# Linear attention, then a gated network, on one core: the first batch's key–value sums in four column groups and two banks, the last two slots in fresh banks by halves, and a new written-out order

## The chip, the cores and the metric

The kernel runs on one core of a Trainium2 chip. The core has TensorE (PE, matmuls; its weight loads are listed apart as PEld), VectorE (DVE), ScalarE (ACT), GpSimd (POOL) and SyncE (SP, which here only issues DMAs). Each takes its own instructions in order and waits on semaphores for the others. Matmuls write to PSUM, of which this kernel uses eight banks of 512 float32 per partition. The metric is the device time of one execution in microseconds (us); lower is better.

## The reference

Four batches, four heads, 1088 tokens, 32 features per head. `phi` makes 64 features of 32, as the outer product of two projections to 8. The attention is linear: per batch and head a 64×32 matrix `kv` and a vector `z` are summed over the tokens, then divided out per token. The result, 4352 tokens × 128, goes through a root-mean-square norm and a gated network with 1536 hidden units.

```python
def phi(x):
    a = np.einsum('rd,bhsd->bhsr', S1, x)
    b = np.einsum('rd,bhsd->bhsr', S2, x)
    return np.einsum('bhsi,bhsj->bhsij', a, b).reshape(*x.shape[:-1], r * r)
q_p, k_p = (phi(q), phi(k))
kv = np.einsum('bhsf,bhsd->bhfd', k_p, v)
z = np.sum(k_p, axis=2)
num = np.einsum('bhsf,bhfd->bhsd', q_p, kv)
den = np.einsum('bhsf,bhf->bhs', q_p, z)[..., None] + 1e-06
...
rms = np.sqrt(np.mean(x * x, axis=-1, keepdims=True) + 1e-06)
xn = x / rms * rms_g
g = xn @ w_gate
silu = g * (1.0 / (1.0 + np.exp(-g)))
val = xn @ w_val
return (silu * val @ w_out).astype(np.float32)
```

## The kernel before

The work is written as some 1280 small tasks, each with the engine or engines that can take it, what it reads and what it writes. The order in which the tasks go to the engines' queues is a list of task numbers (`ORDER`), and a string (`ON`) says which engine takes a task that has a choice. A planner (`Plan.follow`) walks this list with estimated durations, only to interleave the queues, to give out buffers, and to place a few filling matmuls at the start; on the chip each engine's queue has the order of the list, and semaphores do the rest.

**Keys** (`kside`, one call per batch). The keys of a batch come as nine tiles of 128 tokens, in groups (`K0` for batch 0, four groups; `KN` for the others, three). For a group, TensorE multiplies the keys with S1 and S2 (L479), the result is copied (`both` or `kab`, L306 and L307) and VectorE or GpSimd forms the features `phi` as a broadcast product (L434). Then the key–value matmuls (L490) add up `kv` and `z` over the tiles, with the features as the stationary operand and 34 columns of values as the moving one. In the batches listed in `QUARTERS` (1, 2, 3) a matmul takes 32 features, and four neighbours write to four column groups; batch 0 takes 64 features to a matmul. Two copies (`put`, L501 on VectorE, or L505 on ScalarE), one for the even heads and one for the odd, take the sums out of PSUM. In batch 0 the sums lie in the bank `o_ps`, in the others in one of the three `att` banks.

**Queries** (`qside`, one call per chunk of 512 tokens, the ninth of 256). Chunks 0 and 1 form their features with the tokens on the partitions (products L543, L434) and transpose them (L551); their products share one buffer, `at`, so chunk 1's wait for chunk 0's transposes. Later chunks go through DRAM (`far`, L571 to L600). Then come the numerator matmuls (L620), the denominator (L637, with EPS added), its reciprocal (L638), the division (L629), the mean of squares (L644), a root on GpSimd (`rstd`, L657), the scaling (`xn`, L660 or L677), a transpose (L664), and the split into `x_hi` (ScalarE, L667) and `x_lo` (VectorE, L670).

**Weights** (`weights`, one call for each of twelve blocks). The weights arrive as 64-bit words and are turned into float32 by an absolute value on ScalarE (L359) and four steps on VectorE (clamp L343, shift L347, sign L351, join `w_f` L354), and then split into `w_hi` (ScalarE, L415) and `w_lo` (VectorE or GpSimd, L418).

**Slots** (`slot`, one for each chunk and block, 108 in all). A slot is a gate and a value product of three passes each (L714), a silu (L723), a product `h` (L726), a split into `h_hi` and `h_lo` (L741, L744) and a down product of three passes into `o_ps` (L752). The first four slots and the last two (`LAST_EXACT`) take the down product in plain float32 (L733) instead. A chunk's twelve slots add up in the single bank `o_ps`; chunks 0 and 1 are done in two runs of six slots, the first of which is copied to `part` and added at the end (L768). The very last slot is worked in halves of 128 columns: gate and value products, `h`, down product, the copy to `o_sb` (L306, L307) and the store (L779; the first half from SyncE's queue, the second from ScalarE's).

The banks are: three `att`, one `o_ps`, two `g_ps` and two `v_ps`.

Of the kernel before, what the change touches and what calls it, by code (L numbers as in the profile page):

```python
# [12 lines left out]
U32 = mybir.dt.uint32  # L13
# [31 lines left out]
K0 = [(0, 1), (1, 4), (4, 6), (6, 9)]  # L45
# [39 lines left out]
"""  # L85
ON = (
    "daddpadadadadaadaaaaddappadpaddappappadpaddadpadpapdappadapadaaapaddaaddaapadapddaaddapdddddadpddpdddpdddddadddadaapddpd"
    "ddpdddpdppaaaddapppddpdppdppdaappddpppppppdpdpadappdpddddpddpdpdaadddddpdppddpdddpaaappapppppddpddppdppdddpddppad"
)
ATT = 3  # L90
QUARTERS = (1, 2, 3)
KEY1 = 1
KAB = 9
QHALVES = 1
# [7 lines left out]
STALLS = (4500, 900), (12000, 800)  # L102
# [33 lines left out]
class Plan:  # L136
# [32 lines left out]
    def follow(self, clock0, filler):  # L169
# [6 lines left out]
        for i in map(int, ORDER.split()):  # L176
# [28 lines left out]
            if e == "dma":  # L205
                wire = max(wire, at + FLIGHT) + w.lat
                while stalls and wire > stalls[0][0]:
                    wire += stalls.pop(0)[1]
                t.end = wire + SETTLE
                if not w.since:  # L210
                    landed.append(t.end)
            else:
                t.end = at + lat
# [45 lines left out]
def attention_then_glu(ctx, tc, kT, v, qT, sw, w, out):  # L259
# [128 lines left out]
    load(P * NB * 8, lambda: nc.scalar.dma_start(out=s_raw.rearrange("p n c -> p (n c)"), in_=sw.bitcast(U32)), ["s_raw"], since=740)  # L388
# [56 lines left out]
    def kside(b):  # L445
# [24 lines left out]
        for i, (lo, hi) in enumerate(groups):  # L470
            m, ab = hi - lo, gate(i % 2) if first or b <= KEY1 else ps("att", ATT)
            if not i:
                acc = ps("o_ps", 1) if first else ps("att", ATT)

# [9 lines left out]
            def kvmm(lo=lo, hi=hi):  # L484
                kvv = acc()[:, :2 * VA].rearrange("p (a x) -> p a x", x=VA)
                for t in range(lo, hi):
                    for h in range(H):
                        for f in range(0, F, wide):
                            r0 = (h % 2) * F + f
                            nc.tensor.matmul(  # L490
                                out=kvv[r0:r0 + wide, h // 2, :], lhsT=phi()[:, t, h * F + f:h * F + f + wide], rhs=vt()[:, t, h, :],
                                start=(t == 0 and h < 2), stop=(t == KT - 1), skip_group_check=True,
                            )
# [3 lines left out]
            pe(123 * m + 75 if b in QUARTERS else 232 * m + 10, kvmm, [(phi, i), *of(vt, vpieces, lo, hi)], [acc], None, 32 if b in QUARTERS else 64)  # L497
        for hh in range(2):
            def put(rows=slice(hh * F, (hh + 1) * F), xs=slice(hh * (D + 1), (hh + 1) * (D + 1))):
# [356 lines left out]
```

## Time and profile before

| | |
|---|---|
| median of three runs | 261.37 us (259.86 to 261.77) |
| the profiled execution, own time | 259.89 us |
| its span in the profile | 258.1 us |
| TensorE busy | 252.1 us, 98% of the span, 2120 matmuls |
| VectorE, ScalarE, GpSimd busy | 168.7 us, 147.8 us, 91.9 us |
| moved by DMA | 22.13 MB |
| TensorE clock granted | 0.998 |

All times in the profile count from the start of the span. A row of the timeline gives the start, the duration, the engine, the source line, the operation, what is written and read, the shapes, and how many equal neighbours were put together; in brackets stands how long the engine had been idle before it and what released it. Instructions of one engine overlap a little, so the step from one start to the next is often less than the duration. A row of stretches gives the borders, the length, and then the busy time and number of instructions of each engine shown (in the order PE, PEld, DVE, ACT, POOL), the granted clock, the share of DMA time and GB/s.

### The profile page before, as it was taken

The page shows a single profiled execution, that of the slowest core. Times are in us where ns is not written, and L with a number is a line of the kernel's source. Part 1 is how long each engine was busy: PE and PEld are TensorE (multiplying, and loading weights), DVE is VectorE, ACT ScalarE, POOL GpSimd, SP SyncE. Part 2 cuts the span into 40 slices and gives each one's busy share as a digit, 9 for nine tenths or more (in the row PEclk, how much of TensorE's full clock was granted, in tenths as well). Part 3 has the DMA queues.
Part 4 walks back from the last instruction along what each step waited for, and adds up shares of the span by engine and source line. Part 5 has one row for each costly group of instructions (what it writes and reads, how often), then busy time and mean ns, then how long its engine had stood idle before and what let it go on. Part 6 is the DMA issues. An engine that isn't in the chain of part 4 may idle for free.

```text
span 258.1 us, 5584 instructions
## 1 busy us (share of the span) xinstructions
PE 252.1 (98%) x2120; PEld 203.6 (79%) x2120; DVE 168.7 (65%) x396; ACT 147.8 (57%) x319; POOL 91.9 (36%) x93
## 2 busy tenths in 40 slices
PE   7899999999999999999999999999999999999995
PEld 4777688788788787887888788788888878888894
DVE  2999999998697675548466556456855655435552
ACT  3587798467644546544566617546645655547651
POOL 2331131204743303544525544531332126252421
PEclk9999999999999999999999999999999999999999
DMA  7969994064051161061151300000000100010010
GB/s 234 397 243 291 296 353 103 3 207 120 1 171 35 63 161 26 1 167 38 23 144 33 102 20 3 0 21 22 1 0 0 42 3 0 0 41 3 0 41 22
DMA packets 13498, 22.13 MB, mean 86 GB/s; under 512 B 1952, under 2 KB 5024, under 8 KB 13472
## 3 DMA queue, kind: packets, MB, share of 16 engines
q1 hardware_dynamic: 13040, 21.52, 26.8%
q8 instruction: 16, 0.26, 0.4%
q10 hardware_dynamic: 432, 0.26, 0.3%
q14 instruction: 10, 0.08, 0.1%
HBM read 18.69 MB, written 3.08 MB: 84 GB/s over the span
## 4 chain that ended last, share of the span: by engine, by line
PE 94%; DVE 3%; DMA 1%; issue 1%; ACT 0%
PE g_ps L714 28%; PE v_ps L714 28%; PE o_ps L752 26%; PE att L620 3%; PE o_ps L733 2%; PE att L664 2%; PE att L490 2%; DMA s_raw<-sw 1%; PE att L571 1%; PE att L479 1%; DVE at L434 1%; PE att L543 0%; PE g_ps L479 0%; DVE w_tmp L343 0%; DVE w_tmp L347 0%
## 5 line engine op out<-in xcount | busy, mean ns | idle before, releaser
L726 DVE TENSOR_TENSOR h<-v_ps,s 128x512 f32<-128x512 f32 (+2 forms) x109 | 70.0, 652 | 48.2 <-PE v_ps L714 26.3
L744 POOL TENSOR_TENSOR h_lo<-h,h_hi 128x512 fp32r<-128x512 f32 (+1 forms) x48 | 58.9, 1235 | 92.0 <-ACT h_hi L741 42.7
L723 ACT ACTIVATE s<-g_ps 128x512 f32<-128x512 f32 (+1 forms) x108 | 60.7, 572 | 45.6 <-PE g_ps L714 30.8
L741 ACT CAST h_hi<-h 128x512 fp32r<-128x512 f32 (+1 forms) x102 | 59.8, 598 | 43.5 <-DVE h L726 39.2
L714 PE MATMUL v_ps<-x_hi,w_hi 128*128 128x512 f32 (+2 forms) x111 | 43.8, 394 | 0.0
L714 PE MATMUL g_ps<-x_hi,w_hi 128*128 128x512 f32 (+2 forms) x111 | 43.2, 389 | 0.0
L744 DVE TENSOR_TENSOR h_lo<-h,h_hi 128x512 fp32r<-128x512 f32 (+1 forms) x54 | 35.0, 661 | 11.8 <-POOL h_lo L744 5.9
L714 PE MATMUL g_ps<-x_lo,w_hi 128*128 128x512 f32 (+2 forms) x111 | 41.9, 378 | 0.0
L714 PE MATMUL v_ps<-x_hi,w_lo 128*128 128x512 f32 (+2 forms) x111 | 41.8, 377 | 0.0
L714 PE MATMUL v_ps<-x_lo,w_hi 128*128 128x512 f32 (+2 forms) x111 | 41.8, 377 | 0.0
L714 PE MATMUL g_ps<-x_hi,w_lo 128*128 128x512 f32 (+2 forms) x111 | 41.8, 377 | 0.0
L752 PE MATMUL o_ps<-h_hi,w_hi 128*128 128x512 f32 (+1 forms) x102 | 39.5, 387 | 0.0
L752 PE MATMUL o_ps<-h_lo,w_hi 128*128 128x512 f32 (+1 forms) x102 | 39.2, 384 | 0.0
L752 PE MATMUL o_ps<-h_hi,w_lo 128*128 128x512 f32 (+1 forms) x102 | 39.1, 383 | 0.0
L714 PEld LDWEIGHTS v_ps<-x_hi,w_hi 128*128 128x128 f32 x111 | 20.9, 188 | 5.5 <-DVE h L726 0.7
L714 PEld LDWEIGHTS g_ps<-x_hi,w_hi 128*128 128x128 f32 x111 | 20.9, 188 | 4.7 <-ACT w_hi L415 0.2
L714 PEld LDWEIGHTS v_ps<-x_hi,w_lo 128*128 128x128 f32 x111 | 20.9, 188 | 4.4 <-issue 0.7
L714 PEld LDWEIGHTS g_ps<-x_lo,w_hi 128*128 128x128 f32 x111 | 20.9, 188 | 4.2
L714 PEld LDWEIGHTS g_ps<-x_hi,w_lo 128*128 128x128 f32 x111 | 20.9, 188 | 4.2 <-DVE w_lo L418 0.2
L714 PEld LDWEIGHTS v_ps<-x_lo,w_hi 128*128 128x128 f32 x111 | 20.8, 188 | 4.2
L752 PEld LDWEIGHTS o_ps<-h_lo,w_hi 128*128 128x128 f32 x102 | 19.2, 188 | 4.0
L752 PEld LDWEIGHTS o_ps<-h_hi,w_hi 128*128 128x128 f32 x102 | 19.2, 188 | 3.8
(96 smaller groups left out, 255.4 us busy)
## 6 DMA issues: line engine op xcount, KB each, us to landing
w_raw<-w SPq DMA_DIRECT2D x12, 384.0 KB
bt<-far SPq DMA_DIRECT2D x24, 128.0 KB
at<-far SPq DMA_DIRECT2D x12, 256.0 KB
outT<-o_sb SPq DMA_DIRECT2D x8, 256.0 KB
q<-qT SPq DMA_DIRECT2D x7, 256.0 KB
vt<-v SPq DMA_DIRECT2D x4, 272.0 KB
kt<-kT SPq DMA_DIRECT2D x4, 256.0 KB
vt<-v SPq DMA_DIRECT2D x3, 340.0 KB
```

The costliest lines, as they stand in the source:

```text
L434: eng.tensor_tensor(out=out().rearrange("p t (h i j) -> p (t h) i j", h=H, i=R), in0=a[:, :, 0, :].unsqueeze(3).to_broadcast([P, m * H, R, ...
L479: nc.tensor.matmul(out=ab()[n0:rows.stop, (t - lo) * HALF:(t - lo + 1) * HALF], lhsT=kt()[:, s0:s0 + len(rows)], rhs=sblk, start=True, sto ...
L490: nc.tensor.matmul(out=kvv[r0:r0 + wide, h // 2, :], lhsT=phi()[:, t, h * F + f:h * F + f + wide], rhs=vt()[:, t, h, :], start=(t == 0 and ...
L620: nc.tensor.matmul(out=nv[n0:rows.stop, t, p, :], lhsT=phi()[:, p, l0:l0 + len(rows)], rhs=kvs[cut][:, p, :], start=True, stop=True,)
L664: nc.tensor.transpose(out=xt()[:, t * P:(t + 1) * P], in_=xn()[:, t, :], identity=ident)
L714: nc.tensor.matmul(out=acc()[:, cs], lhsT=wt[:, j, i3, :], rhs=x()[:, cs], start=(i == 0), stop=(i == 2))
L723: act(n, lambda: nc.scalar.activation(out=s()[:, :n], in_=gps()[:, :n], func=AF.Silu), cols(gps, whole[0]), [s])
L726: cs.stop - cs.start, lambda cs=cs: nc.vector.tensor_tensor(out=h()[:, cs], in0=vps()[:, cs], in1=s()[:, cs], op=ALU.mult),
L733: (cs.stop - cs.start) * 1.676 + 4, lambda cs=cs: nc.tensor.matmul(out=o_ps()[:, cs], lhsT=w_f[:, j, 2], rhs=h()[:, cs], start=first, stop ...
L741: act(n, lambda: nc.scalar.copy(out=h_hi()[:, :n], in_=h()[:, :n]), hs, [h_hi], True)
L744: eng.tensor_tensor(out=h_lo()[:, :n], in0=h()[:, :n], in1=h_hi().bitcast(F32)[:, :n], op=ALU.subtract)
L752: nc.tensor.matmul(out=o_ps()[:, :n], lhsT=wt[:, j, 2, :], rhs=x()[:, :n], start=first and i == 0, stop=last and i == 2,)
```

## The change

Batch 0 joins `QUARTERS`: its key–value matmuls take 32 features each, so there are twice as many. Its sums lie in two banks, `o_ps` for the even heads and an `att` bank for the odd ones; the two copies read one bank each. The groups of batch 0 are now tiles 0, 1 to 3, 4 to 6, 7 to 8 (the last two were 4 to 5 and 6 to 8).

The last chunk is done in two runs: slots 0 to 9 in `o_ps`, copied to `part`, and slots 10 and 11 in two `att` banks, one for each half of 128 columns. In both these slots `h` and the down product are made by halves; the gate and value products of the last slot are whole again. The end is two additions on VectorE (each a half from its own bank plus the same half of `part`) instead of two copies.

The denominator may go to ScalarE (10 of 17 do). `ORDER` and `ON` are new throughout; the planner's constants for stalls and for one load change with them, which only touches the interleaving. Read by task names, the order of the first slots' preparation is:

| engine | before | after |
|---|---|---|
| TensorE, key–value part | products of q1.2; kv tiles 0, 1–3, 4–5, 6–8; numerators of chunk 0; transposes of q1 | transposes of q0; kv 0, 1–3; transpose of q1.0; kv 4–6, 7–8; transpose of q1.2; numerators of chunk 0 |
| TensorE, ahead of the first slot | products of batch 1's keys and of tiles 0–2 of batch 2 | products of batch 1's keys |
| VectorE, up to the reciprocals | products q0.2, k0.0, q0.0, k0.2, k0.3, q1.2; weight 1 (clamp to join), copy out of kv, denominators, weight 0 (clamp, shift) | products q0.0, k0.1, k0.3, clamp 0, q1.0, k0.2; weights 0 and 1 (shift to join), weight 2 (clamp, shift) |
| ScalarE | one copy out of kv | both copies out of kv, denominators of chunks 0 and 1, each behind a rounding of a weight |
| loads from SyncE, after q1 | values, weight 1, values, values, weight 0, keys 1 | weight 0, values, weight 1, values, values, weight 2, keys 1 |

```diff
-K0 = [(0, 1), (1, 4), (4, 6), (6, 9)]
+K0 = [(0, 1), (1, 4), (4, 7), (7, 9)]
...
-QUARTERS = (1, 2, 3)
+QUARTERS = (0, 1, 2, 3)
 KEY1 = 1
 KAB = 9
+DEN_ACT = 60
...
-STALLS = (4500, 900), (12000, 800)
+STALLS = ((4500, 600), (12000, 400))
+SLATE = 650
...
                 acc = ps("o_ps", 1) if first else ps("att", ATT)
+                accs = [acc, ps("att", ATT) if first else acc]
...
-                kvv = acc()[:, :2 * VA].rearrange("p (a x) -> p a x", x=VA)
+                views = [a()[:, :2 * VA].rearrange("p (a x) -> p a x", x=VA) for a in accs]
                 for t in range(lo, hi):
                     for h in range(H):
+                        kvv = views[h % 2]
...
-            dve(20, lambda view=view, den=den: nc.vector.tensor_scalar_add(den(), view()[:, :, D:D + 1], EPS), [num], [den])
+            plan.add({
+                "dve": on_dve(20, lambda view=view, den=den: nc.vector.tensor_scalar_add(den(), view()[:, :, D:D + 1], EPS)),
+                "act": on_act(20, lambda view=view, den=den: nc.scalar.activation(
+                    out=den(), in_=view()[:, :, D:D + 1], func=AF.Copy, bias=EPS), against=DEN_ACT),
+            }, [num], [den])
...
-    runs = [(c, range(*r)) for r in ((0, CUT), (CUT, NJ)) for c in range(2)] + [(c, range(NJ)) for c in range(2, len(CHUNKS))]
+    runs = [(c, range(*r)) for r in ((0, CUT), (CUT, NJ)) for c in range(2)] + [(c, range(NJ)) for c in range(2, len(CHUNKS) - 1)]
+    runs += [(len(CHUNKS) - 1, r) for r in (range(NJ - LAST_EXACT), range(NJ - LAST_EXACT, NJ))]
...
-        up, rest_of = halves if t < 2 or not left else whole, halves if not left else whole
+        up, rest_of = halves if t < 2 else whole, halves if left < LAST_EXACT else whole
...
         if first:
-            acc_o[c] = ps("o_ps", 1)
-        o_ps = acc_o[c]
+            acc_o[c] = [ps("att", ATT) for _ in halves] if left < LAST_EXACT else [ps("o_ps", 1)]
+        o_ps, o_of = acc_o[c][0], acc_o[c]
...
-            for cs in rest_of:
+            for cs, o in zip(rest_of, o_of):
                 pe(
-                    (cs.stop - cs.start) * 1.676 + 4, lambda cs=cs: nc.tensor.matmul(
-                        out=o_ps()[:, cs], lhsT=w_f[:, j, 2], rhs=h()[:, cs], start=first, stop=last and cs.stop == n
+                    (cs.stop - cs.start) * 1.676 + 4, lambda cs=cs, o=o: nc.tensor.matmul(
+                        out=o()[:, cs], lhsT=w_f[:, j, 2], rhs=h()[:, cs], start=first, stop=last
...
-            dve(
-                n, lambda: nc.vector.tensor_tensor(out=o_sb()[:, :n], in0=o_ps()[:, :n], in1=part()[:, :n], op=ALU.add),
-                [*done, part], cols(o_sb, whole[0]),
-            )
+            for cs, o in zip(rest_of, o_of):
+                dve(
+                    cs.stop - cs.start, lambda cs=cs, o=o: nc.vector.tensor_tensor(out=o_sb()[:, cs], in0=o()[:, cs], in1=part()[:, cs], op=ALU.add),
+                    [*cols(o, cs), part], cols(o_sb, cs),
+                )
```

More of the change, by code (lines that the diff above doesn't have):

```diff
@@ L48 @@
 ORDER = """
[36 rows of a table removed]
[36 rows of a table added]
 """
 ON = (
-    "daddpadadadadaadaaaaddappadpaddappappadpaddadpadpapdappadapadaaapaddaaddaapadapddaaddapdddddadpddpdddpdddddadddadaapddpd"
-    "ddpdddpdppaaaddapppddpdppdppdaappddpppppppdpdpadappdpddddpddpdpdaadddddpdppddpdddpaaappapppppddpddppdppdddpddppad"
+    "ddpadadadaaadaapaaaaaaddappaddapdaddaddadpapdadpaddaddappapadapaaadaapaaaaddaadapapadadddaaaddpddpadppdpddpddddaddpapada"
+    "adddaadpddpdppddppaaadpadddppddppdppdpdaapdadappppddddddpdadapdadaddpddpppdpdpdadpdddapdpdppddppppadadpdadppppppddpddadp"
+    "pppddpdpa"
 )
 ATT = 3
-QUARTERS = (1, 2, 3)
+QUARTERS = (0, 1, 2, 3)
 KEY1 = 1
 KAB = 9
+DEN_ACT = 60
 QHALVES = 1
@@ L208, in follow @@
                     wire += stalls.pop(0)[1]
-                t.end = wire + SETTLE
+                t.end = wire + SETTLE + (w.occ - ISSUE if w.since else 0)
                 if not w.since:
@@ L386, in s_join @@
         nc.vector.tensor_tensor(out=sblk.bitcast(U32), in0=s_tmp.bitcast(U32), in1=s_top, op=ALU.bitwise_or)
-    load(P * NB * 8, lambda: nc.scalar.dma_start(out=s_raw.rearrange("p n c -> p (n c)"), in_=sw.bitcast(U32)), ["s_raw"], since=740)
+    plan.add({"dma": Way(
+        ISSUE + SLATE, P * NB * 8 / 320, lambda: nc.scalar.dma_start(out=s_raw.rearrange("p n c -> p (n c)"), in_=sw.bitcast(U32)), since=740
+    )}, (), ["s_raw"])
     plan.add({"act": Way(1500, 1500, lambda: nc.scalar.activation(out=spare, in_=mhalf, func=AF.Silu))}, (), ["table"])
@@ L496, in kside, with put, put_act @@
             product(lambda lo=lo, hi=hi: phi()[:, lo:hi], ab, m, [(phi, i)], not first)
-            pe(123 * m + 75 if b in QUARTERS else 232 * m + 10, kvmm, [(phi, i), *of(vt, vpieces, lo, hi)], [acc], None, 32 if b in QUARTERS else 64)
+            pe(123 * m + 75 if b in QUARTERS else 232 * m + 10, kvmm, [(phi, i), *of(vt, vpieces, lo, hi)], list(dict.fromkeys(accs)), None, 32 if b in QUARTERS else 64)
         for hh in range(2):
-            def put(rows=slice(hh * F, (hh + 1) * F), xs=slice(hh * (D + 1), (hh + 1) * (D + 1))):
+            def put(rows=slice(hh * F, (hh + 1) * F), xs=slice(hh * (D + 1), (hh + 1) * (D + 1)), acc=accs[hh]):
                 kvv = acc()[:, :2 * VA].rearrange("p (a x) -> p a x", x=VA)
                 nc.vector.tensor_copy(out=kv[rows, :, xs], in_=kvv[rows, :, :D + 1])
-            def put_act(rows=slice(hh * F, (hh + 1) * F), xs=slice(hh * (D + 1), (hh + 1) * (D + 1))):
+            def put_act(rows=slice(hh * F, (hh + 1) * F), xs=slice(hh * (D + 1), (hh + 1) * (D + 1)), acc=accs[hh]):
                 kvv = acc()[:, :2 * VA].rearrange("p (a x) -> p a x", x=VA)
                 nc.scalar.copy(out=kv[rows, :, xs], in_=kvv[rows, :, :D + 1])
-            plan.add({"dve": on_dve(2 * (D + 1), put), "act": on_act(2 * (D + 1), put_act, against=PUT_ACT)}, [acc], [("kv", b, hh)])
+            plan.add({"dve": on_dve(2 * (D + 1), put), "act": on_act(2 * (D + 1), put_act, against=PUT_ACT)}, [accs[hh]], [("kv", b, hh)])
     xs, qs = {}, {}
@@ L730, in slot @@
         if t < EXACT or left < LAST_EXACT:
-            for cs in rest_of:
+            for cs, o in zip(rest_of, o_of):
                 pe(
-                    (cs.stop - cs.start) * 1.676 + 4, lambda cs=cs: nc.tensor.matmul(
-                        out=o_ps()[:, cs], lhsT=w_f[:, j, 2], rhs=h()[:, cs], start=first, stop=last and cs.stop == n
+                    (cs.stop - cs.start) * 1.676 + 4, lambda cs=cs, o=o: nc.tensor.matmul(
+                        out=o()[:, cs], lhsT=w_f[:, j, 2], rhs=h()[:, cs], start=first, stop=last
                     ),
-                    [("w_f", j)] + cols(h, cs), [*cols(o_ps, cs), (o_ps, "group")], due, 0,
+                    [("w_f", j)] + cols(h, cs), [*cols(o, cs), (o, "group")], due, 0,
                 )
```

72 rows, old and new, of the table ORDER are left out of this document.

## The prediction

> **What bounds the kernel now.** I read the page's busy shares and its chain first, then the busy time of each engine in three stretches cut at two instants of the TensorE timeline: the first matmul of a slot (18.78) and the last matmul's end (255.06).
>
> ```profile
> PE 252.1 (98%) x2120; PEld 203.6 (79%) x2120; DVE 168.7 (65%) x396; ACT 147.8 (57%) x319; POOL 91.9 (36%) x93
> PE 94%; DVE 3%; DMA 1%; issue 1%; ACT 0%
> 4.00:18.78 14.78, 12.64 (x295) 10.49 (x293) 12.98 (x47) 8.61 (x29) 5.02 (x5) 1.00 0.90 332
> 18.78:255.06 236.28, 236.26 (x1814) 191.22 (x1812) 155.31 (x348) 137.39 (x288) 85.63 (x78) 1.00 0.23 69
> 255.06:258.10 3.04, 0.00 (x0) 0.00 (x0) 0.29 (x1) 0.27 (x1) 0.00 (x0) 0.87 0.17 46
> ```
>
> In a row of stretches the first number is its length, the second TensorE's busy time. In the long middle stretch TensorE is busy 236.26 of 236.28 us at full clock (1.00): nothing there waits. So the end is a sum of three: when the first slot starts, plus all TensorE work from then on, plus the tail. An edit pays only if it starts the slots earlier, takes TensorE work out of the middle, or shortens the tail.
>
> What sets the start is read in the timeline of the first 19 us: the chain of chunk 0 from the division to the first slot.
>
> ```profile
> 13.59 0.20 DVE L638 RECIPROCAL rden<-den 128x8 f32<-128x8 f32 x1
> 14.84 0.55 DVE L351 SCALAR_TENSOR_TENSOR w_tmp<-w_raw,w_tmp 128x384 uint32<-128x384 uint32 x1
> 15.30 0.28 DVE L644 CUSTOM_DVE_ANT_0 sq<-x 128x128 f32<-128x128 f32 x1
> 15.51 0.55 DVE L354 SCALAR_TENSOR_TENSOR w_f<-w_raw,w_tmp 128x384 uint32<-128x384 uint32 x1
> 15.98 0.28 DVE L644 CUSTOM_DVE_ANT_0 sq<-x 128x128 f32<-128x128 f32 x1
> 15.67 1.75 POOL L657 TENSOR_TENSOR rstd<-ms,mhalf 128x2 f32<-128x2 f32 x2 [5.32 <-DVE ms L644]
> 17.67 0.69 ACT L677 ACTIVATE xn<-x,rstd 128x128 f32<-128x128 f32 x2
> 18.27 0.46 ACT L667 ACTIVATE x_hi<-att,gain_t 128x256 fp32r<-128x256 f32 x1
> 18.78 0.39 PE L714 MATMUL v_ps<-x_hi,w_hi 128*128 128x256 f32 x1
> ```
>
> VectorE takes two weight conversions (L351 at 14.84, L354 at 15.51) between the divisions and the means. GpSimd's two roots wait for those means, ScalarE's second scaling (17.67) for the second root, and x_hi and the first slot follow at once.
>
> **The start, part by part.** The first batch's key–value pass:
>
> ```profile
> 9.36:11.60 2.24, 2.24 (x72) 2.13 (x72) 1.00 1.05 411
> 50.87:52.24 1.37, 1.37 (x144) 1.26 (x144) 1.00 0.20 31
> 8.45 0.95 DVE L434 TENSOR_TENSOR phi<-v_ps,both 128x768 f32<-128x768 f32 x1
> 12.14 0.21 ACT L505 COPY kv<-o_ps 64x66 f32<-64x66 f32 x1 [1.83 <-DVE kv L501]
> 12.40 1.16 PE L620 MATMUL att<-kv,phiq 128*64 128x66 f32 x32 [0.80 <-ACT kv L505]
> ```
>
> Before, 72 instructions take 2.24 us (31 ns each). Batch 1, in 32-feature matmuls, takes 144 in 1.37 us (9.5 ns each). The pass therefore shrinks by 0.87 us, at best by 1.55 (to half of 1.37), on the other side rival (d). But its last features bind too. The old order's last product ends at 9.40 (8.45 + 0.95, 768 wide; so about 0.65 for 512 and 0.35 for 256). Its products are named by chunk or batch and piece (q1.0: queries of chunk 1, first half; k0.2: keys of batch 0, third group). The new VectorE list is q0.0, k0.1, k0.3, one weight step, q1.0, k0.2: against the old one it holds a weight step (0.27, below) and q1.0 (0.65) more and k0.0 (0.35) less, 9.97, and q1.0 must wait for the transposes that read its buffer; I take 10.2. The five tiles behind (80 instructions of 9.5 ns, and the change of shape) end near 11.2. Both copies out go to ScalarE, in two banks; of the old pair ScalarE's waited for VectorE's (its row names L501) and ended at 12.35. Two copies of 0.21 and the hops behind 11.2 put the numerator matmul at 11.75 instead of 12.40, a gain of 0.65.
>
> Nothing of this gain reaches the reciprocal by itself.
>
> ```profile
> 23.28 0.35 DVE L343 TENSOR_SCALAR w_tmp<-w_tmp 128x384 f32<-128x384 f32 x1
> 23.55 0.55 DVE L354 SCALAR_TENSOR_TENSOR w_f<-w_raw,w_tmp 128x384 uint32<-128x384 uint32 x1
> ```
>
> A short weight step holds VectorE for 0.27 (23.28 to 23.55), a long one for 0.47 (15.51 to 15.98 above). Nine of them stand between k0.2 and the reciprocal (four long, five short, and 0.2 for steps that follow their own input: 3.4 us), so the reciprocal starts near 13.65, as before (13.59). The gain appears because those steps stand there: the two conversions that followed the division (0.46 + 0.47 = 0.93) are now ahead of it. By my count the first two means end at 15.1, GpSimd starts its roots at 15.2 (15.67), the second half of 1.75 later at 16.1 (16.55), ScalarE's second scaling runs at 17.05 (17.67), x_hi at 17.65, the first slot at 18.15. That is −0.6. On the good side the numerator alone could set it: its old distance to the slot, 18.78 − 12.40 = 6.38, less 0.93, gives 17.2 (−1.55). On the bad side the gain is nothing, or the last rival's loss.
>
> The denominators of chunks 0 and 1 move to ScalarE (L637, about 0.2 us each). They stand behind weight roundings that wait for VectorE's conversion. The first numerators end near 12.35 (11.75 and half of 1.16); the roundings ahead wait for conversions that end near 12.1 and 13.1 by the nine steps and take 0.3 each; so I count the two done at 12.7 and 13.6, just in time for 13.65; if that cover goes, each 0.1 us is 0.1 us of start.
>
> The loads are reordered, weight 0 ahead of the values, so weight 1 comes later:
>
> ```profile
> 8.79 0.56 ACT L359 ACTIVATE w_tmp<-w_raw 128x384 f32<-128x384 f32 x1
> 8.00:10.00 2.00, 1.92 (x40) 1.78 (x40) 1.79 (x4) 1.69 (x5) 1.31 (x2) 1.00 1.03 396
> w_raw<-w SPq DMA_DIRECT2D x12, 384.0 KB
> ```
>
> Weight 1 had landed by 8.79 and waited for nothing there. One more 384 KB at 396 GB/s puts it at most 1.0 later, 9.8. ScalarE, in order, then holds three copies (0.5 each) and the two copies of kv until 12.1: 0.35 more than my 11.75, hidden by the nine weight steps. I cost it at nothing.
>
> **TensorE work in the middle.** One matmul group moves behind the first slot (the products of batch 2's keys with S1 and S2, tiles 0 to 2); it used to sit in the wait for x:
>
> ```profile
> 18.08 0.52 PE L479 MATMUL att<-sblk,kt 128*64 128x64 f32 x12
> 18.53 0.44 PE L664 MATMUL att<-ident,xn 128*128 128x128 f32 x2
> ```
>
> Twelve instructions, 18.08 to 18.53 with the change of tile shape: +0.4 (bounds 0.35 and 0.45). The attention pieces behind the first slot stand in 10 groups instead of 11, and entering and leaving one costs:
>
> ```profile
> 52.24 0.90 PE g_ps L714 x3
> 53.14 0.69 PE v_ps L714 x3
> ```
>
> three slot matmuls take 0.90 instead of 0.69 behind such a group: −0.1 to −0.2, I take −0.1. The last slot's gate and value products become whole:
>
> ```profile
> 245.48 0.22 PE L714 MATMUL g_ps<-x_hi,w_hi 128*128 128x128 f32 x1
> 245.76 0.34 PE L714 MATMUL g_ps<-x_hi,w_hi 128*128 128x256 f32 x1
> 246.53 0.28 PE L714 MATMUL v_ps<-x_hi,w_hi 128*128 128x256 f32 x1
> 246.89 0.28 PE L714 MATMUL v_ps<-x_hi,w_hi 128*128 128x256 f32 x1
> 251.56 0.22 PE L714 MATMUL v_ps<-x_hi,w_hi 128*128 128x128 f32 x1
> 252.18 0.33 PE L714 MATMUL g_ps<-x_hi,w_hi 128*128 128x256 f32 x1
> ```
>
> Three passes over a half take 0.28 (245.48 to 245.76), two halves of the value product 0.62 (251.56 to 252.18), a whole product 0.36 (246.53 to 246.89). So 0.56 + 0.62 − 2 × 0.36 = −0.46. Slot 10's down product splits into two halves of the same columns: nothing. The rest of the order shuffles equal work; it costs only if something is then late (rivals).
>
> **The tail.**
>
> ```profile
> 254.01 1.04 PE L733 MATMUL o_ps<-h,w_f 128*128 128x256 f32 x6
> 255.08 0.27 ACT L306 COPY o_sb<-o_ps 128x128 f32<-128x128 f32 x1 [1.85 <-PE o_ps L733]
> 255.38 0.29 DVE L307 COPY o_sb<-o_ps 128x128 f32<-128x128 f32 x1 [1.49 <-ACT o_sb L306]
> 255.70 0.35 ACTq L779 DMA_DIRECT2D outT<-o_sb  x1
> ```
>
> Both halves share a bank, so ScalarE's copy waits for the last matmul and VectorE's for ScalarE; the last store is issued 0.64 after the matmul. Now half 0 is finished two matmuls earlier and in its own bank, and half 1 is added by VectorE directly behind its last matmul: 0.02 + 0.29 + 0.03, store issued at 0.34. −0.3, bounded by 0 and −0.35. The partial sum of slots 0 to 9 (one ScalarE copy, about 0.4) lies beside the last 0.86 us of matmuls; without that cover it would cost up to 0.4.
>
> **Sum.** −0.6 + 0.4 − 0.1 − 0.46 − 0.3 = −1.06. The profiled execution took 259.89 (span 258.1 and 1.79 around it), so its like would take 258.8. It is the low one of three; the median, 261.37, stands 1.48 above it. I carry the difference to the median: 260.3.
>
> **Rivals.** (a) *The start pays more*: the numerator binds as worked out above, −1.55 instead of −0.6, 259.4. For it: the reciprocal's place depends on my guess for VectorE's steps. (b) *VectorE binds the early slots*, and an earlier start turns into TensorE waits:
>
> ```profile
> 30.00:38.00 8.00, 8.00 (x32) 5.82 (x31) 7.71 (x17) 6.50 (x16) 2.46 (x3) 1.00 1.03 360
> 38.00:46.00 8.00, 8.00 (x36) 6.40 (x35) 7.97 (x16) 6.04 (x15) 1.27 (x3) 1.00 0.46 108
> ```
>
> VectorE is busy 7.71 and 7.97 of 8 us, TensorE 8.00 of both. Against it: VectorE issues 13 tasks fewer, ten of them denominators. The −0.6 is lost: 260.9. (c) *Slower: a weight arrives late.* TensorE takes its queue in order; in the new order weight 9 is converted before weight 6, so one weight can come a whole conversion late, two steps of 0.47 and two of 0.27, 1.5 us, and every slot behind waits. With (b) that is −0.46 + 1.5 = +1.04, 262.4. It decides once VectorE's queue lags TensorE's order by more than its present slack, which the trace doesn't show since TensorE never waits. (d) *The four column groups don't overlap*, so the change doesn't do what it says: batch 0 alternates between two banks, which no traced pass does. 144 instructions at 31.1 ns are 4.48 us, 3.1 more than forecast; the start moves from −0.6 to about +2.2 (0.3 is hidden by the weight steps): 263.1.
>
> The Trainium skill, TensorEngine Tiling, Instruction Overhead, speaks for (d): each matmul has an overhead of about 60 cycles, so one of few columns is no faster than one of 60, and a tiling factor shouldn't come out of a dimension already small. By that rule doubling these 34-column matmuls would double the pass; the 9.5 ns of batch 1 against 31 ns contradict it where neighbours go to different column groups.
>
> **How the numbers follow.** Forecast 0.58, (a) 0.14, (b) 0.15, (c) 0.09, (d) 0.04. Runs of one kernel here lie 259.86 to 261.77, so about 1% (2.6 us) is what a measurement can tell from no change. The range takes in (a), (b) and (c), and below (a) the low run: 258.6 to 262.4. Faster by over 1% would need 258.8: (a) with a low run, or the forecast with one, 0.13; slower by over 1% only (d) or (c) with a high run, 0.04; else 0.83.
>
> **What would show it.** The pass of batch 0: 144 instructions, and its last stretch at about 10 ns each. First slot at 18.15. TensorE idle under 0.3 us from there to its last matmul. Two adds on VectorE at the end, the last store 0.35 behind the last matmul. It is wrong if TensorE shows waits between 20 and 50 us, or if ScalarE's denominators hold the reciprocal past 13.9.

## Result and the profile after

The changed kernel took 262.16 us in the median (261.80 to 263.83, 15 runs), the kernel before, on the same chip, 261.39 (259.86 to 261.93, 15 runs). The ratio is 1.0052, 95% interval 1.0033 to 1.0071: half a per cent **slower**, where 260.3 and a gain of 0.4% were forecast. The ratios here and below go by all runs (means 262.43 and 261.04) and not by the medians: the kernel before runs near 260.05 (as in its profiled execution, 259.89) or near 261.4, and its median falls in either group. The median lies inside the forecast's range, at its upper end, but on the other side of the kernel before, and none of the prediction's rivals is the cause.

The busy shares and the queue of TensorE's own code, on the page of the changed kernel. That kernel has 151 more instructions (5735 against 5584).

```profile
span 260.3 us, 5735 instructions
PE 252.7 (97%) x2188; PEld 203.9 (78%) x2188; DVE 163.2 (63%) x383; ACT 152.5 (59%) x343; POOL 95.0 (36%) x93
q8 instruction: 17, 0.28, 0.4%
PE 94%; issue 1%; DVE 1%; DMA 1%; ACT 1%; DVEq 0%
```

The three stretches of the prediction, cut at the same two instants (first slot, end of the last matmul); the columns are as there.

```profile
4.00:21.75 17.75, 13.75 (x355) 10.80 (x353) 12.69 (x42) 9.92 (x37) 4.89 (x6) 0.90 0.88 335
21.75:257.52 235.77, 235.77 (x1820) 191.21 (x1820) 149.79 (x340) 141.12 (x306) 88.80 (x77) 1.00 0.22 65
257.52:260.30 2.78, 0.00 (x0) 0.00 (x0) 0.29 (x1) 0.00 (x0) 0.00 (x0) 0.95 0.17 47
```

The middle is 235.77 instead of 236.28 us, still without a TensorE wait, and the tail 2.78 instead of 3.04: together 0.77 won. But the first slot starts at 21.75 instead of 18.78: 2.97 lost. The sum is +2.2, the difference of the two spans. So the whole question lies in the start. Its TensorE rows in the timeline (start, length, tile, count, and in brackets the idle time ahead and its releaser):

```profile
10.15 0.22 PE L497 MATMUL o_ps<-vt,phi 128*32 128x34 f32 x2 [0.21 <-DVE phi L439]
...
13.83 0.19 PE L497 MATMUL o_ps<-vt,phi 128*32 128x34 f32 x1 [2.97 <-issue]
...
13.98 0.23 PE L497 MATMUL att<-vt,phi 128*32 128x34 f32 x4
14.15 1.06 PE L558 MATMUL att<-ident,at 128*128 128x128 f32 x4
15.14 2.03 PE L627 MATMUL att<-kv,phiq 128*64 128x66 f32 x32
...
21.75 0.38 PE L726 MATMUL v_ps<-x_hi,w_hi 128*128 128x256 f32 x1
```

The second piece of batch 0's pass runs from 10.15 to 10.86 at about 10 ns an instruction, as forecast. Then, with 21 instructions of the pass left, TensorE stands still for 2.97 us. "issue" means that it waits for nothing that the profile shows. The place says more: 11 of the 32 instructions of the last group (tiles 7 and 8) are done when it stops, so the features and the first of its values are there. And a count of matmul records (one record is one matmul in the trace) up to the stop and up to its end:

```profile
0.00:10.90 10.90, 9.37 (x221) 6.59 (x222) 6.16 (x17) 5.93 (x17) 4.07 (x13) 1.00 0.83 309
0.00:13.80 13.80, 9.37 (x221) 6.59 (x222) 8.11 (x21) 5.93 (x17) 4.07 (x13) 1.00 0.87 327
```

221 records, in both. Behind the stop the numerators (15.14) take 2.03 instead of 1.16 us, since the granted clock is halved (the column ahead of the last two; TensorE alone):

```profile
14.00:14.50 0.50, 0.50 (x23) 0.76 1.07 406
14.50:15.00 0.50, 0.50 (x4) 0.50 1.02 387
...
17.00:17.50 0.50, 0.50 (x16) 0.50 1.00 389
17.50:18.00 0.50, 0.50 (x8) 0.83 1.13 423
```

### The profile page after: what moved, and what is told of

Read it like the earlier page. It is cut to its first block, busy times and chain, and to the rows that moved or that the text cites. A ratio compares the mean times of both kernels' runs of the same rounds, so it can differ in the third digit from the quotient of the medians.

```text
span 260.3 us, 5735 instructions
## 1 busy us (share of the span) xinstructions
PE 252.7 (97%) x2188; PEld 203.9 (78%) x2188; DVE 163.2 (63%) x383; ACT 152.5 (59%) x343; POOL 95.0 (36%) x93
## 4 chain that ended last, share of the span: by engine, by line
PE 94%; issue 1%; DVE 1%; DMA 1%; ACT 1%; DVEq 0%
PE g_ps L726 28%; PE v_ps L726 28%; PE o_ps L764 26%; PE att L627 4%; PE att L497 2%; PE att L675 1%; PE o_ps L745 1%; DMA s_raw<-sw 1%; PE att L485 1%; PE att L578 1%; PE g_ps L485 1%; PE att L558 0%; PE v_ps L485 0%; PE att L550 0%; PE att L745 0%
## 5 line engine op out<-in xcount | busy, mean ns | idle before, releaser
L756 POOL TENSOR_TENSOR h_lo<-h,h_hi 128x512 fp32r<-128x512 f32 (+1 forms) x51 | 62.2, 1230 | 91.1 <-ACT h_hi L753 40.4
L753 ACT CAST h_hi<-h 128x512 fp32r<-128x512 f32 (+1 forms) x102 | 58.8, 598 | 35.1 <-DVE h L738 33.7
L756 DVE TENSOR_TENSOR h_lo<-h,h_hi 128x512 fp32r<-128x512 f32 (+1 forms) x51 | 33.8, 667 | 15.2 <-ACT h_hi L753 12.1
L726 PE MATMUL g_ps<-x_hi,w_hi 128*128 128x512 f32 (+1 forms) x110 | 43.2, 394 | 0.0
L726 PE MATMUL v_ps<-x_hi,w_hi 128*128 128x512 f32 (+1 forms) x110 | 42.1, 383 | 0.0
L726 PE MATMUL g_ps<-x_lo,w_hi 128*128 128x512 f32 (+1 forms) x110 | 41.6, 378 | 0.0
L726 PE MATMUL v_ps<-x_hi,w_lo 128*128 128x512 f32 (+1 forms) x110 | 41.5, 378 | 0.0
L726 PE MATMUL g_ps<-x_hi,w_lo 128*128 128x512 f32 (+1 forms) x110 | 41.5, 377 | 0.0
L726 PE MATMUL v_ps<-x_lo,w_hi 128*128 128x512 f32 (+1 forms) x110 | 41.4, 378 | 0.0
(100 smaller groups left out, 261.6 us busy)
```

The lines of the kernel that those rows point to most:

```text
L726: nc.tensor.matmul(out=acc()[:, cs], lhsT=wt[:, j, i3, :], rhs=x()[:, cs], start=(i == 0), stop=(i == 2))
L753: act(n, lambda: nc.scalar.copy(out=h_hi()[:, :n], in_=h()[:, :n]), hs, [h_hi], True)
L756: eng.tensor_tensor(out=h_lo()[:, :n], in0=h()[:, :n], in1=h_hi().bitcast(F32)[:, :n], op=ALU.subtract)
```

## Experiments

**The theories.** *Code*: TensorE's program comes over its own queue in packets of 16 KB (0.28 MB in 17 packets). I read a packet as a block of 128 matmuls with their 128 weight loads: 2188 matmuls and as many loads in 17 packets are 257 instructions to a packet, and before, 2120 in 16, they are 265. Block edges then lie behind matmul record 221, 349 and so on, and 93 ahead of them (what else fills the first places isn't shown); the next block is taken to be asked for when the one before is entered. With short matmuls TensorE is through a block before the next has come, above all when loads fill the DMA engines (some 400 GB/s and a share of 1.0 in the rows above). *Data*: the third values piece comes late. *Order*: the new order is late by itself. Some matmul records are missing in a trace, so that an edge late in a run is met a few records early by the count.

**1. The changed kernel with batch 0's pass in 64-feature matmuls (72 records fewer).**

```
-QUARTERS = (0, 1, 2, 3)
+QUARTERS = (1, 2, 3)
```

> The changed kernel with one part undone: batch 0 again takes 64 features to a matmul (72 instructions instead of 144 in its key-value pass); two banks, order, tail and denominators stay. In the changed kernel TensorE stands from 10.86 to 13.83 us, 11 instructions into the last 32 of the pass. Theory (code): at that point, after some 222 matmul records and as many weight loads, TensorE has used up the instructions it holds, and the next block of them comes late behind the loads. With 72 pairs fewer ahead of it the edge moves to about the numerators of chunk 1: no stop in the pass, pass over by 11.9, first slot at 18.2 to 19.0, device time 1.5 to 3 us below the changed kernel, 0.2 to 1.5 below before. Rival (data): the stop is the third piece of values, queued behind weight 0 and 1: it stays until 13.8 and the first slot stays above 21. Rival (order): the new order is late by itself: first slot above 20 with no single long stop.

Measured: 263.99 us (263.85 to 264.46), ratio to before 1.0126 (1.0088 to 1.0164). The start came as the code theory has it: no stop in the pass, first slot at 18.56, ahead of the kernel before. The time missed: two new stops came later.

```profile
81.96 0.22 PE L497 MATMUL att<-vt,phi 128*32 128x34 f32 x1 [2.17 <-issue]
146.23 0.33 PE L578 MATMUL att<-q,sab 64*32 64x64 f32 x12 [0.70 <-issue]
```

```profile
78.36 1.42 PE L497 MATMUL att<-vt,phi 128*32 128x34 f32 x143
```

The first is in batch 2's pass, with 143 of its 144 instructions done, at record 982 (221 + 6 × 128 is 989; I take seven records to be missing). So 72 records fewer had moved every later edge, and a whole block of 128 now lay in a pass of 1.42 us. That stretch of the DMA engines is nearly empty (0.14 busy, 38 GB/s), so a block can be late without any load: it was entered near 78.5 and work went on at 81.96, some 3.5 us.

**2. The kernel before with batch 0's pass in 32-feature matmuls**, its own order and loads.

```
-QUARTERS = (1, 2, 3)
+QUARTERS = (0, 1, 2, 3)
```

> The kernel before with one part of the change alone: batch 0 takes 32 features to a matmul, in its one bank, with the old order and the old tail. Theory (code): the old kernel has used 96 matmul records when the pass begins, so an edge at some 222 falls about 126 instructions into the 144: a stop there until about 14, first slot at 21 to 22, span 260 to 261.5, 0.7 to 1.3% slower than before. Rival (data): here the values are loaded ahead of weight 0, so no stop; the pass takes about 1.4 instead of 2.24 us and the span is 257.3 to 258.1, equal or up to 0.3% faster. Rival (the column groups don't overlap): the pass alone takes 4.5 us without a stop.

Measured: 270.48 us (269.3 to 271.3), ratio 1.0368 (1.0319 to 1.0417). Three stops, the first after exactly 221 records:

```profile
14.57 0.38 PE L490 MATMUL o_ps<-vt,phi 128*32 128x34 f32 x19 [2.06 <-issue]
96.36 0.32 PE L490 MATMUL att<-vt,phi 128*32 128x34 f32 x11 [2.27 <-issue]
133.54 0.33 PE L571 MATMUL att<-q,sab 64*32 64x64 f32 x11 [2.01 <-issue]
```

```profile
0.00:14.50 14.50, 10.63 (x221) 1.00 0.89 306
```

So the new order isn't needed for the stop; the narrow pass alone brings it, and two more where its 72 records move the edges to. Those two weren't expected, and so the time missed (a ratio of 1.007 to 1.013 was expected). Part of the late start (first slot at 22.79) isn't the stop's: the pass already begins at 11.14 instead of 9.36, since this execution's early matmuls are slow (the last paragraph of this document).

**3. The changed kernel with 16 half-width warm-up matmuls instead of 8** (a warm-up matmul leaves two records, so 16 more records ahead of the pass, of the same length in all).

```
-    keep_warm(WARM)
+    keep_warm(2 * WARM, n=HALF)
```

> The changed kernel with the 8 filling matmuls at the start replaced by 16 of half the width: the same time, but 16 matmul records and 16 weight loads more ahead of everything else. Theory (code): the stop comes at the same count of instructions, so 16 matmul records earlier in the work, near the end of the third group of the pass (about 37 instead of 21 of its 144 instructions behind the stop); its end stays within 0.7 us of 13.8, time within 0.4% of the changed kernel. Rival (data): the stop stays where it was, 11 instructions into the last group.

Measured: 262.57 us (260.99 to 264.52), ratio 1.0062 (1.0032 to 1.0091). The stop (2.60, ending at 13.97) moved to 37 instructions before the pass's end, 21 + 16, and a second one (1.75, ending at 20.28) stands exactly 128 records behind:

```profile
0.00:11.50 11.50, 9.77 (x221) 1.00 0.86 303
0.00:13.90 13.90, 9.77 (x221) 1.00 0.89 317
0.00:18.50 18.50, 14.02 (x349) 1.00 0.93 337
0.00:20.20 20.20, 14.06 (x349) 1.00 0.89 324
```

A stop that goes with a count of instructions and not with a tile is neither data nor order. The second stop wasn't expected, and the profiled execution (264.52) is the longest of the ten, so it needn't stand in all of them.

**4. The changed kernel with weight 2's load, and what is behind it in SP's queue, held until VectorE has made the features of k0.2** (issued at 10.8 instead of 5.1 us), to give the code packet empty DMA engines. SP's loads are kept in written order. `held` is the task of weight 2's load, task 28 the product of k0.2 (L439 in the changed kernel), `spots` the place of a task's first and last instruction.

```
+    for i in held:
+        tie(made[spots[i][0]], made[spots[28][1]], mybir.DependencyClass.Sync)
...
-        if e not in (ENG.PE, ENG.Activation, ENG.DVE, ENG.Pool):
+        if e not in (ENG.PE, ENG.Activation, ENG.DVE, ENG.Pool, ENG.SP):
```

> The changed kernel with the loads behind the last piece of values (weight 2 and all later ones) held until VectorE has made the features of the third group (about 10.1 us), so that the DMA engines run empty from about 9.5. Theory (code behind loads): the stop stands at the same instruction but ends earlier, at 12.2 or before, because the block of instructions doesn't wait behind the loads. Rival (a fixed delay of the block after it is asked for): the stop still ends near 13.8. The first slot may be late for another reason here, since weight 2 arrives near 13 and ScalarE's queue waits for it; so the reading is the end of the stop, not the time.

Measured: 260.15 us (259.77 to 260.68), ratio 0.9977 (0.9955 to 0.9999). The packet crosses in 9.25 to 9.50 instead of 11.00 to 11.25, and the stop is gone but for 0.3 us; the rows are the code queue's, of the changed kernel and of this one.

```profile
q8 instruction: 1, 0.02, 28.1%
```

```profile
q8 instruction: 1, 0.02, 23.3%
```

Weight 2 is now late, which holds ScalarE and so the second numerators:

```profile
14.16 0.54 ACT L364 ACTIVATE w_tmp<-w_raw 128x384 f32<-128x384 f32 x1 [1.65 <-DMA w_raw<-w]
```

**5 and 6. Shorter holds**, until the product of k0.3 (task 32, weight 2 issued at 8.49), and until the first 64 matmuls of the pass (task 25). The edits are shown against run 4.

```
-        tie(made[spots[i][0]], made[spots[28][1]], mybir.DependencyClass.Sync)
+        tie(made[spots[i][0]], made[spots[32][1]], mybir.DependencyClass.Sync)
...
+        tie(made[spots[i][0]], made[spots[25][1]], mybir.DependencyClass.Sync)
```

> The changed kernel with weight 2's load, and the loads behind it, held only until the coefficients of the last keys piece (about 8.0 us) instead of 10.8 as in the run with the loads held. Code theory: TensorE asks for the block behind matmul record 221 when it enters the block before it, at record 93 (about 8.5 us here), so loads released at 8.0 are partly ahead of that request: a stop of 0.3 to 1.5 us at record 221, shorter than the 2.97 us of the changed kernel; weight 2 is in time; first slot at 18.8 to 19.8, time 259.2 to 260.5. Rival (the stop is the work of the data, whatever the code): the third values piece is loaded ahead of weight 2 in both, so the hold does no more here than in the longer hold, and the stop is gone in both alike.

Measured (5): 259.29 us (258.67 to 259.72), the kernel before beside it 260.28, ratio **0.9935 (0.9910 to 0.9959)**. Each of its nine runs is below the lowest of the kernel before (259.82), so this version beats both kernels. Stop 0.49, first slot 19.24, no half clock: inside each bound of the code theory.

```profile
11.93 0.19 PE L499 MATMUL o_ps<-vt,phi 128*32 128x34 f32 x1 [0.49 <-issue]
...
12.83 1.16 PE L629 MATMUL att<-kv,phiq 128*64 128x66 f32 x32
...
19.24 0.39 PE L728 MATMUL v_ps<-x_hi,w_hi 128*128 128x256 f32 x1
```

> The same with the loads held until the first 64 matmuls of batch 0's kv pass are done (about 8.9 us), just behind the request for the block. Code theory: the code packet lands before 10 us as in the longer hold, the stop at record 221 is at most 0.4 us, the clock stays up, weight 2 lands near 12.5 rather than 14.2 us and is no longer late; first slot at 18.2 to 19.0 and a time of 258.5 to 259.6, under both the changed kernel (262.2) and the kernel before (261.4). Rival (it is only that the start has less traffic): no better than the longer hold, 260.2.

Measured (6): 259.36 us (258.68 to 260.87), ratio 0.9955 (0.9932 to 0.9977). The time came as expected, the steps did not: the load was issued at 9.85, not 8.9, the stop was 0.78, a second of 0.81 came at record 349, and the profiled execution (260.87, the slowest of the 12) had its first slot at 20.50. So the exact moment of the release is not settled by these two.

**7. Run 1 with 72 records of padding** (36 more narrow warm-up matmuls, two records each) at 13.9 us, so that the later edges fall as in the changed kernel.

```
-        for _ in range(k):
...
+        n = 8 if len(calls) == 3 else P
+        for _ in range(37 if len(calls) == 3 else k):
...
```

> The changed kernel with batch 0's kv pass at 64 features again (72 matmul records fewer), and with 72 records of padding (36 more narrow warm-up matmuls) put at about 13.8 us, behind record 221, so that all later block edges fall where they fall in the changed kernel. Code theory: no stop in the pass; the stops of 2.17 us at 82 and 0.70 us at 146, which the 64-feature run had and the changed kernel has not, vanish; the padding costs 0.5 to 1.5 us at the start (first slot at 19.0 to 20.1), and the span comes to 258.8 to 260.2 against 262.1 without the padding. Rival (the later stops come with the order or with the 64-feature pass by itself): they stay, and the padding makes the time longer by its own 0.5 to 1.5 us: a span of 262.6 to 263.6.

Measured: 262.97 us (261.09 to 265.02), ratio 1.0071 (1.0039 to 1.0102), span 261.6. Both late stops vanished, as the code theory said. The time missed it and the first slot too (21.48): the 74 narrow matmuls run in 2.00 us, so the block that ends at record 349 was through early, while loads filled the DMA engines, and the stop came there.

```profile
13.94 2.00 PE L341 MATMUL v_ps<-const-float32-0.0 128*1 128x8 f32 x74
...
20.00 0.55 PE L582 MATMUL att<-q,sab 64*32 64x128 f32 x16 [2.28 <-issue]
```

**8 and 9. Controls**: a hold of like length in the kernel before (weight 2's load behind the product of k0.2, task 28; issued at 10.06 instead of 6.82), and the changed kernel with SP's loads in written order but nothing held (the second change alone).

```
+    tie(made[plan.spots[89][0]], made[plan.spots[28][1]], mybir.DependencyClass.Sync)
...
-        if e not in (ENG.PE, ENG.Activation, ENG.DVE, ENG.Pool):
+        if e not in (ENG.PE, ENG.Activation, ENG.DVE, ENG.Pool, ENG.SP):
```

> The kernel before, with the same hold as in the short hold of the changed kernel: weight 2's load waits until the coefficients of the keys piece that ends at 8.5 us (it was issued at 6.8). It has no stop of TensorE at its first block edge (record 221 falls near 15.3 us, with the code packet there since 11.75), so by the code theory the hold has nothing to win: first slot at 18.6 to 19.4, time 260.0 to 261.2, ratio to before 0.999 to 1.004. Rival (the hold is worth something by itself, whatever the block edges): 259.0 to 259.6 here too, ratio 0.995 to 0.997.

> The changed kernel with its SP loads kept in the written order, as in all runs with the loads held, but nothing held. The code theory expects the stop of 2.3 to 3.0 us at record 221 and the half clock behind it as in the changed kernel, and 261.5 to 262.7. Rival (the order of the queue, not the hold, took the stop away): no stop and 259.0 to 260.2.

Measured: (8) 260.08 us, before 260.09, ratio 1.0004 (0.9982 to 1.0026): the hold is worth nothing where no stop is (the first slot of the profiled execution, 20.39, missed the 18.6 to 19.4 that was expected; its early matmuls are slow). (9) 262.8 (261.42 to 263.6), ratio 1.0101 (1.0068 to 1.0134), with the stop at record 221 again:

```profile
13.90 0.19 PE L497 MATMUL o_ps<-vt,phi 128*32 128x34 f32 x1 [2.42 <-issue]
```

So it is the hold, not the queue's order, that takes the stop away. The half clock that the code theory expected did not come in the profiled execution, the shortest of the five (below); the mean clocks of the other four, 0.987 to 0.993, say that it came there.

**Starts and ends together**, each from the profiled execution. Runs 1, 2, 3 and 7, which have stops or the half clock behind the first slot, are left out; kv0.1 is tiles 1 to 3 of the pass.

| kernel | first slot | span | span less first slot |
|---|---|---|---|
| before | 18.78 | 258.1 | 239.3 |
| before, hold (8) | 20.39 | 259.8 | 239.4 |
| changed | 21.75 | 260.3 | 238.6 |
| changed, written order (9) | 21.19 | 259.6 | 238.4 |
| changed, long hold (4) | 19.95 | 258.4 | 238.5 |
| changed, hold to k0.3 (5) | 19.24 | 257.8 | 238.6 |
| changed, hold to kv0.1 (6) | 20.50 | 259.1 | 238.6 |

Behind the first slot the change is worth 0.7 to 1.0 us against the kernel before in every one of these; the first slot's place decides the rest.

## Why the prediction was wrong

The step that failed is **the first slot at 18.15, "−0.6"**; it came at 21.75, 3.60 later than forecast and 2.97 later than before. Inside it, the term that failed is the end of the pass, "80 instructions of 9.5 ns … end near 11.2". The last features came as forecast (the second piece begins at 10.15, forecast 10.2), and the duration of an instruction was right. What the sum put at nothing, without a reason, is a wait for TensorE's own instructions: 2.97 us, and the half clock behind it. With these put in, the forecast closes: 11.75 for the numerators, plus 2.97, plus 0.40 for the transposes ahead of them (0.99 us from start to start, against 0.59 in (9), which has the stop and no half clock) is 15.12, and 15.14 was measured; from there to the slot it took 6.61, where 6.4 was forecast.

Batch 1's pass, from which the 9.5 ns were read, showed them at one position of the code edges and with few loads beside it (a DMA share of 0.20); 9.5 ns a matmul also means 128 of them in 1.2 us, and nothing in the sum asked whether TensorE's program comes that fast. The page of before had the queue: 16 packets.

```profile
q8 instruction: 16, 0.26, 0.4%
```

In before, matmul 221 falls near 15.2 us, some 3.5 behind the packet seen at 11.50 to 11.75, and TensorE shows no wait there; the count of records:

```profile
0.00:15.33 15.33, 12.42 (x224) 1.00 0.90 329
```

In the change it falls at 10.86, with the packet at 11.00 to 11.25 and work going on 2.6 to 2.8 later; (5) and (6) show nearly the same distance (2.4 to 2.7). What the loads add, by this reading, is the time ahead of the packet: about 2.9 us from entering the block (near 8.2) in the changed kernel, 0.5 in (5). The DMA engines were busy in (5) too just then (381 GB/s from 8.50 to 9.00), so it would be the loads already queued that count and not the traffic of the moment; no run separates the two.

The Trainium skill, Runtime: NRT & Kernel Launch, Instruction fetch mechanics, says that each engine's program comes in 16 KiB blocks of 256 instructions, that the sequencer fetches the next while it runs the present one, and that crossing a block edge is "mostly hidden". The block size agrees with the 128 records, each a matmul and a weight load, between the stops of run 3; that it is hidden does not, by 2.97 us here.

**Right**: the chain behind the pass. The forecast had numerators at 11.75, the reciprocal 1.9 later and the slot 6.4 behind the numerators (18.15). In (5), where the stop is 0.49 and the pass begins 0.58 later than in the changed kernel (8.84 against 8.26), numerators are at 12.83, 1.08 later than forecast, and the slot at 19.24, 6.41 behind them. So with the stop and the later start put in, the forecast slot is 18.15 + 1.07 = 19.22. In run 1, where no stop is, the reciprocal starts at 13.84 (forecast 13.65). The gain of that chain is right only as a distance: the 0.6 has been seen in no run in full, and nearest in run 1 (18.56, which has the slower pass).

**The tail**, −0.3: measured −0.26.

```profile
256.46 1.06 PE L745 MATMUL att<-h,w_f 128*128 128x128 f32 x8
...
257.17 0.68 DVE L781 TENSOR_TENSOR o_sb<-att,part 128x128 f32<-128x128 f32 x2 [0.98 <-ACT part L309]
257.48 0.33 SPq L792 DMA_DIRECT2D outT<-o_sb  x1
257.88 0.35 ACTq L792 DMA_DIRECT2D outT<-o_sb  x1
```

The last store is issued at 257.88, 0.36 behind the last matmul's end (257.52), 0.34 by the forecast.

**The middle**, −0.16 (+0.4 − 0.1 − 0.46): measured −0.51. The group did move behind the slot, and the last slot's products are whole; which term is 0.35 too small was not taken apart.

**The rivals.** (d) is refuted: the column groups overlap in two banks. (a) needed the slot about 5.45 behind the numerators (6.38 less 0.93); it is 6.41 in (5). (b) and (c) did not come: TensorE is busy 235.77 of 235.77 us. ScalarE's denominators did hold the reciprocal in the changed kernel, but there the numerators were late, behind the stop and under the half clock: its row is

```profile
16.54 0.20 DVE L649 RECIPROCAL rden<-den 128x8 f32<-128x8 f32 x1 [0.50 <-ACT den L646]
```

and in (5) and run 1 that reciprocal (14.70 and 13.84) shows no such wait.

**The step to the median**, +1.48, was wrong too, and it hid most of the miss. It carried the distance between the profiled execution of the kernel before and its median over to the changed kernel, which has no such distance (262.07 and 262.16). Profile against profile the forecast was 258.8 and the result 262.07, 3.3 us more; that 262.16 still lies inside 258.6 to 262.4 is luck.

With the stop mostly out of the way, (5) is 0.65% under before (0.41 to 0.90%, 1.1 to 2.3 us), at least the 1.06 that was forecast, but not by the forecast's parts: in its profile the first slot (19.24) is still 0.46 behind before's 18.78, and what is won lies behind it. So the parts behind the first slot are better in sum than forecast and the chain is as long as forecast, but the gain of the start isn't shown.

## What to carry to other kernels

A duration per instruction read from one stage is only half a price: ask also how fast the instructions themselves arrive. Once one stop put down to "issue" inside a group of equal matmuls is found, count on from it: here the next edges lay at steps of 128 matmuls. Splitting work into more, shorter matmuls moves every later edge, so one stop removed can come back 60 us further on. Where an edge must fall in such a pass, keep loads from queueing up when the block ahead of it is entered: issuing one load at 8.49 instead of 5.12 us, and all later ones of its queue behind it, took the median from 262.16 to 259.29 here.

## What the runs showed of the hardware

**A block's lead.** From entering a block to work in the next: about 5.6 us with full DMA engines (changed kernel), 3.1 with the loads held (5), some 3.5 with few transfers (run 1, at 82 us). Of this, 2.2 to 2.8 us lie between the packet (in run 1 seen at 79.50 to 79.75) and the work in all three; what TensorE does in that time isn't shown. A block of 34-column matmuls in column groups is done in 1.2 to 1.4 us, so a stop is to be expected where a whole block lies in such a pass.

**The clock behind a stop.** Stops of 2.97 (changed), 2.17 (run 1, at 82) and 2.28 (7) were followed by some 3.5 us at a granted clock of 0.50. One of 2.42 (9) was not, nor one of 2.60 (run 3), whose clock fell only behind the second. In run 2 the stop of 2.06 was, those of 2.27 and 2.01 were not. A row of each stretch of TensorE behind the stop, first of run 1, then of (9):

```profile
84.00:85.00 1.00, 1.00 (x4) 0.50 0.00 0
```

```profile
14.50:15.00 0.50, 0.50 (x10) 1.00 1.03 391
```

So the length alone doesn't decide. The Trainium skill, TensorE: Matmul & The Clock Gate, Why this matters for your kernels, warns of gaps over about 3 us; here it came behind 2.06 and 2.17. That the Trainium skill calls the clock's window free-running (same page, What's actually happening) could explain that equal stops differ; no run here tests it.

The half clock isn't what made the change slower in the median. The mean clock of each execution is on record: of the 15 of the changed kernel three kept 1.00 (261.80 to 261.98 us), nine have 0.992 or 0.993 (261.85 to 262.47) and three 0.987 (263.57 to 263.83). By an estimate from the 3.5 us above, one spell at half clock makes a mean of 0.993 and two make 0.987. So the executions without any are only some 0.3 us shorter than those with one spell (medians 261.85 and 262.16), and still above the 261.39 of the kernel before.

**Early matmuls that take longer at a granted clock of 1.00.** The profiled executions of the kernel before (259.89) and of (8) (261.54) differ from the first matmuls on; the same four warm-up records, before and in (8):

```profile
6.34 0.60 PE L334 MATMUL att<-const-float32-0.0 128*1 128x128 f32 x4
```

```profile
7.36 1.01 PE L336 MATMUL att<-const-float32-0.0 128*1 128x128 f32 x4
```

In (8) the first slot is 1.61 later, and the time 1.65 longer. Run 2's profile has the same long row (1.01, at 7.35). What makes these matmuls slow isn't shown.
